# Unit 3's convolution moved from TensorE to the tap-by-tap path of the other units

## The chip, the cores and the metric

The kernel runs on one core of a Trainium2 chip. The metric is device time of one execution in microseconds (us); of several runs the median is given. A profile is one more execution, recorded by the hardware. Engines are named as in the profile: PE (TensorE matmuls), PEld (its weight loads), DVE (VectorE), ACT (ScalarE), POOL (GpSimd), SP (the sync engine, which only issues DMAs here).

## The reference

`x` has 8 sequences of 4096 tokens with 192 channels. First a causal convolution over 7 tokens: each of 8 heads has 24 channels and 7 weights, which are softmaxed. Then a gated feed-forward layer over all 32768 tokens:

```
w = exp(weight - max); w = w / (sum(w) + 1e-9)          # 8 x 7
y[b, s, h, :] = sum over k of w[h, k] * x[b, s + k - 6, h, :]
g = y @ w_gate; val = y @ w_val                          # 192 -> 1536
out = (g * sigmoid(g) * val) @ w_out                     # 1536 -> 192, float32
```

## The kernel before

**The main loop.** The 32768 tokens are cut into 64 blocks of 512, and the 1536 hidden features into 12 chunks of 128. One step is one chunk of one block, so there are 768 steps. A step `n` does six matmuls in `gate_val` (two halves of 64 rows for gate and val, three slices of the 192 channels), a SiLU on ACT (`sig`, L789) out of the gate's PSUM bank, and a product with val on DVE (`h`, L791). Gate and val have three PSUM banks each. Every third step a `slot` does 24 matmuls of the down projection (L806) on `h` of earlier steps; once a block, ACT and DVE copy the two result banks to `o_sb` and SP stores them.

**Where the convolved input comes from.** `gate_val` needs the convolved block with channels in partitions. Four blocks make a unit of 2048 tokens (48 steps); there are 16 units, 0 to 15. There are three ways to make them:

- Unit 0 (`early`): convolved on PE and turned in part on PE.
- Units 1 and 3: x is loaded in float16 windows of tokens by the POOL queue (`x16_tile`, `load_x`, L98) and duplicated by SP (`dup_x`, L148). `conv_half`, twice a unit, runs 32 matmuls (L476, 64 x 32 tiles of the array) between two groups of a slot's down projection, and casts the banks to `tm` on ACT and DVE (L493). POOL copies 64 channels (`conv_dup`, L504), SP stores `tm` to DRAM (`conv_out`) and fetches it transposed (`fetch`, L534).
- Units 2 and 4 to 15 (the tuple `POOLED`): channel-major, tap by tap. A DMA on the POOL queue casts the unit's x into DRAM as float16 (`cast_x`, L590). SP fetches it transposed, two tiles of 128 channels per block (`turn_x`, L605); the tiles of two blocks are joined for the last 64 channels (`join_x`, L609). Six jobs a unit (`conv_job`: four blocks, two pairs) then do the seven taps: ACT three (L682), DVE two (L657), POOL two products (L647) and four adds (L632). SP puts the results into the tiles that the matmuls read (`place`, L706, four DMAs a block).

**What sets the order.** All engines run a fixed order, written step by step in the loop; `seq` keeps it. For the pooled units `planned(v)` writes into `plan` at which step the cast, the ten turns and joins, and the jobs of unit `v` are handed out. Jobs go to one queue for ACT and one for DVE. `pooled_work` takes from them only in steps with `j` of 1, 7 or 10 (ACT also at 4, and twice at 10 in even blocks), and takes nothing in a step that holds `conv_half`: in four blocks that is at most 12 DVE taps and 18 ACT taps, which is what one unit needs. POOL's part of a job is issued when its DVE and ACT taps are. A block is placed when both its jobs were issued some steps ago and at the earliest 16 steps ahead of it:

```
if n < max(done + (12 if u == 2 else 18), ustep * u + NCH * i - 16):
```

**Buffers.** Tiles come from rings: `x01` and `x12` 8, `pxc0` 8, `pxc1` and `pxc2` 4, `total` 5, `part` 8, `y2` 4, the cast's DRAM buffer `xs` 2, `x16` 2. An instruction that would write a buffer still in use waits, and holds up what stands behind it on its engine or queue.

Of the kernel before, what the change touches and what calls it, by code (L numbers as in the profile page):

```python
# [10 lines left out]
def kernel(  # L11
# [11 lines left out]
    fp16 = mybir.dt.float16  # L23
# [7 lines left out]
    B, S, D = x.shape  # L31
# [3 lines left out]
    P = 128  # L35
# [10 lines left out]
    NG = 10  # L46
# [3 lines left out]
    ER = ((0, 3), (3, 5))  # L50
    XW = 2 * EG * EO
    NU = NT // UT
    POOLED = (2, *range(4, NU))
    upb = S // UT
    n_blocks = NT // TB
    n_steps = n_blocks * NCH
# [25 lines left out]
    cpool = ctx.enter_context(tc.tile_pool(name="conv", bufs=2))  # L82
# [41 lines left out]
    x16 = {}  # L124

    def x16_tile(u):
        x16[u] = cpool.tile([P, 4 * NG, D], fp16, tag="x16", name="x16")

    def load_x(u, r, after=None, low=0):
        t, t0, w0, p0 = x16[u], u * UT, 4 * NG * r, Q * r + low  # L130
# [90 lines left out]
    xe_tile(3)  # L221
    xe_load(3)
    x16_tile(1)
    for r in range(2):
        for low in (0, 32):
# [132 lines left out]
    def make_band():  # L358
        for r in range(2):
            for a in range(2):  # L360
                p0 = Q * r + 32 * a
                p1 = Q * r
                seq(
                    nc.gpsimd.tensor_copy(
                        band[p0 : p0 + 32], wide[p1 : p1 + 32, a, :, 0:32]
                    )
                )
# [208 lines left out]
    def cast_x(u):  # L576
        rows = XP + UT
        xs[u] = dpool.tile([rows, D], fp16, tag="xs", name="xs")
        flat = xs[u].rearrange("t d -> (t d)")
        skip = XP if u % upb == 0 else 0  # L580
        if skip:
            seq(
                nc.sync.dma_start(
                    out=flat[0 : XP * D].rearrange("(a n) -> a n", n=P),
                    in_=fill[0 : XP * D // P, :],
                )
            )
        n = (rows - skip) * D // P
        seq(
            nc.gpsimd.dma_start(  # L590
                out=flat[skip * D : rows * D].rearrange("(a n) -> a n", n=n),
                in_=bass.AP(
                    tensor=x_flat.tensor,
                    offset=(u * UT - XP + skip) * D,
                    ap=[[n, P], [1, n]],
                ),
            )
        )

    def turn_x(u, i, at):  # L600
        rows = xs[u][TB * i : TB * i + TB + XP]
        tiles = (x01, x12)[at // Q]
        tag = f"x{at // Q}"
        t = cpool.tile([P, TB + XP], fp16, tag=tag, name=tag, bufs=8)
        seq(nc.sync.dma_start_transpose(out=t, in_=rows[:, at : at + P]))  # L605
        tiles[u, i] = t

    def join_x(u, i):
        seq(nc.sync.dma_start(out=x12[u, 2 * i + 1][0:Q], in_=x12[u, 2 * i][Q:P]))  # L609
# [98 lines left out]
    def pooled(u):  # L708
        return u in POOLED

# [3 lines left out]
    def queue_jobs(u):  # L714
        for job in (
            ("block", 0), ("pair", 0), ("block", 1),
            ("block", 2), ("pair", 1), ("block", 3),
        ):
            conv_job(u, *job)
        placing.extend((u, i) for i in range(UB))  # L720

    def planned(v):
        s0 = ustep * v
        turns = (
            (0, 0), (0, Q), (1, Q), None, (1, 0), (2, 0), (2, Q), (3, Q), None, (3, 0)
        )
        if v == 2:
            cast, jobs = 21, 55
            times = (36, 36, 36, 38, 39, 39, 41, 41, 43, 43)
        elif v == 3:  # L730
            cast, jobs = 60, 56
            times = range(66, 86, 2)
        else:
            cast, jobs = s0 - 115, s0 - 89
            times = range(s0 - 105, s0 - 85, 2)
        plan.setdefault(cast, []).append(lambda: cast_x(v))
        for m, turn in enumerate(turns):
            if turn:
                todo = lambda turn=turn: turn_x(v, *turn)
            else:  # L740
                todo = lambda i=m // 8: join_x(v, i)
            plan.setdefault(times[m], []).append(todo)
        plan.setdefault(jobs, []).append(lambda: queue_jobs(v))
# [151 lines left out]
    make_band()  # L895
    for v in POOLED:
        planned(v)

    for n in range(n_steps):
        b, j = divmod(n, NCH)  # L900
        u, ls = divmod(n, ustep)
# [50 lines left out]
        if u + 2 < NU and not pooled(u + 2):  # L952
            if ls == (21 if u == 0 else 1):
                x16_tile(u + 2)
                load_x(u + 2, 0, silu[n - 1])
            if ls == (23 if u == 0 else 5):
                load_x(u + 2, 1, silu[n - 1])
            if ls == (37 if u == 0 else 26):
                dup_x(u + 2)
# [44 lines left out]
```

## Time and profile before

| What | Value |
|---|---|
| Time, median of 3 runs | 775.95 us (775.26 to 776.23) |
| Profiled execution | 775.12 us, of it 773.3 us span from the first to the last instruction |
| Granted TensorE clock | 1.00 |
| One half of `conv_half`, PE matmuls | 32, 0.67 us together |
| ACT tap, DVE tap | 715 ns, 1064 ns mean |
| POOL product, add of an ACT part, add of a product | 916 ns, 1271 ns, 1424 ns mean |
| Casts in DRAM (`xs`) | 13, of 768 or 774 KB, median 7 us to landing |

Views of the profile have one line for a group of like instructions or for a few in a row. In a list in order of time a line begins with start and length in us, then engine, source line, operation, what it writes and reads, and how many; what stands in brackets is how long the engine was idle before it and what ended that. "SPq" and "POOLq" are queues that issue DMAs: their lengths are the time to issue. A stretch by engine gives the busy time of PE, PEld, DVE, ACT and POOL in that order with the numbers of instructions, then the clock, the share of the DMA engines and GB/s.

### The profile page before, as it was taken

How to read it: one execution, taken by the hardware profiler on the slowest of the kernel's cores; microseconds unless marked ns; L12 is line 12 of the kernel's file. 1: busy time of each engine (PE TensorE's matmuls, PEld its weight loads, DVE VectorE, ACT ScalarE, POOL GpSimd, SP SyncE). 2: the span in 40 equal slices, each digit the busy share in tenths (PEclk: the TensorE clock that was granted, in tenths of full speed). 3: DMA queues.
4: the chain of work that ended last, by engine and by line, in shares of the span. 5: the costliest groups of instructions: out<-in, count | busy, mean ns of one | idle time of the engine just before them, and what ended most of it. 6: DMA issues, size and time to landing. Idle time of an engine off the chain costs nothing.

```text
span 773.3 us, 27884 instructions
## 1 busy us (share of the span) xinstructions
PE 766.8 (99%) x11179; PEld 645.5 (83%) x11179; DVE 688.9 (89%) x1034; ACT 636.8 (82%) x1093; POOL 578.8 (75%) x525
## 2 busy tenths in 40 slices
PE   8999999999999999999999999999999999999997
PEld 5666686668888888888888888888888888888886
DVE  7677998899999999999999999999999999997775
ACT  6667888888888888888888888888888888886664
POOL 8100796799989999898989989999899998882000
PEclk9999999999999999999999999999999999999999
DMA  9959855854635436355363543627454352221211
GB/s 134 190 125 135 169 118 108 158 105 101 115 96 113 107 86 106 89 118 115 77 119 84 109 101 80 123 78 122 88 111 111 87 121 74 56 70 39 67 57 42
DMA packets 143652, 79.32 MB, mean 103 GB/s; under 512 B 89146, under 2 KB 143042, under 8 KB 143042
## 3 DMA queue, kind: packets, MB, share of 16 engines
q1 hardware_dynamic: 130690, 61.58, 36.3%
q0 software_dynamic: 12832, 15.96, 13.3%
q8 instruction: 87, 1.43, 0.8%
q14 instruction: 43, 0.35, 0.2%
HBM read 31.92 MB, written 37.83 MB: 90 GB/s over the span
## 4 chain that ended last, share of the span: by engine, by line
PE 99%; ACT 0%; DVE 0%; issue 0%
PE gate L780 47%; PE acc L806 33%; PE val L780 18%; PE warm L880 0%; PE turn L445 0%; PE cv L476 0%; PE cv L387 0%; PE acc L827 0%; ACT tme L405 0%; ACT wide L345 0%; ACT o_sb L972 0%; PE taps L332 0%; DVE spread L312 0%; PE ctap L565 0%; DVE tap L310 0%
## 5 line engine op out<-in xcount | busy, mean ns | idle before, releaser
L791 DVE TENSOR_TENSOR h<-sig,val 128x512 f16<-128x512 f16 x768 | 498.8, 684 | 75.3 <-PE gate L780 51.8
L789 ACT ACTIVATE sig<-gate 128x512 f16<-128x512 f32 x768 | 458.2, 597 | 120.1 <-PE gate L780 71.8
L780 PE MATMUL gate<-pxc,w 64*128 64x512 f16 x1872 | 437.7, 376 | 0.0
L780 PE MATMUL val<-pxc,w 64*128 64x512 f16 x1872 | 437.6, 376 | 0.0
L780 PEld LDWEIGHTS <-w 64*128 64x128 f16 x4608 | 366.1, 110 | 85.2 <-issue 0.9
L806 PEld LDWEIGHTS <-h 64*128 64x128 f16 x6096 | 286.8, 94 | 29.4 <-issue 1.4
L806 PE MATMUL acc<-wo,h 64*128 64x192 f16 x6096 | 308.5, 243 | 0.0
L632 POOL TENSOR_TENSOR total<-total,part 128x512 f32<-128x512 f32 x156 | 198.3, 1271 | 64.7 <-DVE total L657 47.4
L657 DVE SCALAR_TENSOR_TENSOR total<-x,both_taps,total 128x512 f32<-128x512 f16 x156 | 166.0, 1064 | 0.0
L647 POOL TENSOR_SCALAR piece<-x,both_taps 128x512 f32<-128x512 f16 x156 | 142.9, 916 | 0.0
L632 POOL TENSOR_TENSOR total<-total,piece 128x512 f32<-128x512 f32 x78 | 111.1, 1424 | 6.5
L682 ACT ACTIVATE part<-x,both_taps 128x512 f32<-128x512 f16 x156 | 111.5, 715 | 0.0
L780 PE MATMUL val<-xc,w 64*128 64x512 f16 x432 | 102.0, 376 | 0.0
L780 PE MATMUL gate<-xc,w 64*128 64x512 f16 x432 | 101.9, 376 | 0.0
L632 POOL TENSOR_TENSOR pxc<-total,piece 128x512 f16<-128x512 f32 x52 | 66.8, 1285 | 4.3
L682 ACT ACTIVATE total<-x,both_taps 128x512 f32<-128x512 f16 x78 | 55.8, 716 | 0.0
L632 POOL TENSOR_TENSOR y<-total,piece 128x512 f16<-128x512 f32 x26 | 33.1, 1274 | 2.2
L864 DVE COPY o_sb<-acc 128x384 f32<-128x384 f32 x63 | 34.6, 549 | 0.0
L863 ACT COPY o_sb<-acc 128x384 f32<-128x384 f32 x63 | 29.8, 473 | 4.5 <-PE acc L806 4.5
L98 POOL DMA_DIRECT2D x<-in_x_dram x6 | 5.1, 871 | 24.4 <-ACT sig L789 24.4
L504 POOL COPY tm<-tm 128x1280 f16<-128x1280 f16 x2 | 2.5, 1252 | 17.3 <-DVE tm L493 17.3
L590 POOL DMA_DIRECT2D xs<-in_x_dram x13 | 7.2, 557 | 0.0
(67 smaller groups left out, 74.3 us busy)
## 6 DMA issues: line engine op xcount, KB each, us to landing
out_dram<-o_sb SPq DMA_DIRECT2D x63, 384.0 KB
pxc<-pxc SPq DMA_DIRECT2D x104, 64.0 KB
pxc<-y SPq DMA_DIRECT2D x104, 64.0 KB
xs<-in_x_dram POOLq DMA_DIRECT2D x7, 768.0 KB, 7.1
xs<-in_x_dram POOLq DMA_DIRECT2D x6, 774.0 KB, 6.8
x<-in_x_dram POOLq DMA_DIRECT2D x6, 480.0 KB, 10.1
scr<-tm SPq DMA_DIRECT2D x14, 130.0 KB
x<-x SPq DMA_DIRECT2D x26, 66.0 KB
```

Of the source, the lines that this page charges most:

```text
L98: nc.gpsimd.dma_start(out=t[p0 + i0 : p0 + i1, w0 - at : w1 - at, :], in_=bass.AP(tensor=x_flat.tensor, offset=(t0 + size * w0 - pad + i0) ...
L590: nc.gpsimd.dma_start(out=flat[skip * D : rows * D].rearrange("(a n) -> a n", n=n), in_=bass.AP(tensor=x_flat.tensor, offset=(u * UT - XP ...
L632: nc.gpsimd.tensor_tensor(job["dst"] if k == K - 1 else total, total, part, op=ALU.add)
L647: nc.gpsimd.tensor_scalar(part, shifted(k), scalar1=job["tap"][:, k : k + 1], scalar2=1.0, op0=ALU.mult, op1=ALU.mult,)
L657: nc.vector.scalar_tensor_tensor(job["total"], shifted(k), job["tap"][:, k : k + 1], job["total"], op0=ALU.mult, op1=ALU.add,)
L682: nc.scalar.activation(part, shifted(k), AF.Copy, scale=job["tap"][:, k : k + 1])
L780: nc.tensor.matmul(o, w16[m][p0 : p0 + Q, k, e::E], xc[b][k][p0 : p0 + Q, 0:TB], start=(k == 0), stop=(k == SL - 1),)
L789: silu[n] = seq(nc.scalar.activation(sg, g, AF.Silu)).ins
L791: seq(nc.vector.tensor_tensor(hj, sg, v, op=ALU.mult))
L806: nc.tensor.matmul(acc[b][bank][:, s, :], hj[p0 : p0 + Q, ts(2 * bank + s, P)], wo16[p0 : p0 + Q, j, :], start=(not second and j == 0 and ...
L863: seq(nc.scalar.copy(o_sb[:, 0:2, :], acc[b][0]))
L864: seq(nc.vector.tensor_copy(o_sb[:, 2:4, :], acc[b][1]))
```

## The change

Unit 3 joins the pooled units, so `conv_half`, `load_x`, `dup_x`, `conv_out` and `fetch` remain for unit 1 alone, and `x16` needs one buffer. The jobs of unit 2 are handed out at step 46 in place of 55. The branch of `planned` for unit 3 (cast at step 60, turns at 66 to 84, jobs at 56, behind those of unit 2 in the queues) stood in the code before and is now used. For units from 4 on, the turns and joins are handed out 95 to 77 steps ahead of the unit in place of 105 to 87.

```
-    POOLED = (2, *range(4, NU))
+    POOLED = range(2, NU)
...
     def x16_tile(u):
-        x16[u] = cpool.tile([P, 4 * NG, D], fp16, tag="x16", name="x16")
+        x16[u] = cpool.tile([P, 4 * NG, D], fp16, tag="x16", name="x16", bufs=1)
...
         if v == 2:
-            cast, jobs = 21, 55
+            cast, jobs = 21, 46
             times = (36, 36, 36, 38, 39, 39, 41, 41, 43, 43)
         elif v == 3:
             cast, jobs = 60, 56
             times = range(66, 86, 2)
         else:
             cast, jobs = s0 - 115, s0 - 89
-            times = range(s0 - 105, s0 - 85, 2)
+            times = range(s0 - 95, s0 - 75, 2)
```

## The prediction

> **What bounds the kernel now.** I read the busy shares first, then the chain of work that ended last, then TensorE in order of time around unit 3's convolution. After that I read the engines that the change loads: stretches by engine, and ScalarE and the sync queue in order of time where the margins are small.
>
> ```profile
> PE 766.8 (99%) x11179; PEld 645.5 (83%) x11179; DVE 688.9 (89%) x1034; ACT 636.8 (82%) x1093; POOL 578.8 (75%) x525
> PE 99%; ACT 0%; DVE 0%; issue 0%
> ```
>
> TensorE is busy for 766.8 of 773.3 us and is 99% of the chain, so only TensorE time counts, and a new wait that TensorE feels. The other engines are hidden as long as they deliver in time. The next view is TensorE in order of time, with the gate and val matmuls between left out (each line: start, length, engine, line, operation, count).
>
> ```profile
> 112.36 1.21 PE L806 MATMUL acc<-wo,h 64*128 64x192 f16 x24
> 115.29 1.21 PE L806 MATMUL acc<-wo,h 64*128 64x192 f16 x24
> 118.22 0.71 PE L806 MATMUL acc<-wo,h 64*128 64x192 f16 x12
> 118.87 0.67 PE L476 MATMUL cv<-x,band 64*32 64x240 f16 x32
> 119.47 0.67 PE L806 MATMUL acc<-wo,h 64*128 64x192 f16 x12
> ...
> 121.92 0.82 PE L806 MATMUL acc<-wo,h 64*128 64x192 f16 x15
> ```
>
> Three steps of the main loop take 115.29 - 112.36 = 2.93 us, and again 118.22 - 115.29 = 2.93. The three that hold half of unit 3's convolution take 121.92 - 118.22 = 3.70. The starts of the gate matmuls in the whole trace say the same: after step 39 every group of three steps takes 2.93 us except the two with unit 3's convolution, 3.697 each. So from step 39 on there are only two irregularities, and the change removes both.
>
> **What goes.** Two halves of unit 3's convolution, 32 matmuls each. Each half costs 3.697 - 2.933 = 0.764 us of TensorE, together 1.53 us. The 0.67 us length of one matmul group bounds it from below (2 x 0.67 = 1.34), and the period difference, which also holds the switch of tile shape and the stop between, is the upper end. I take the period difference because the period is what repeats. Also gone with unit 3, all hidden before: 8 casts on DVE and ACT (0.65 and 0.56 us each), a copy on POOL (1.25 us), two loads of 480 KB on the POOL queue, two duplications, nine stores and twelve transposes on SP. Their cover was the TensorE period, so they give nothing by themselves.
>
> **What comes.** Unit 3 now takes 18 ScalarE taps (0.715 us), 12 DVE taps (1.064), 6 x 4 adds and 6 x 2 products on POOL, a cast in DRAM, 8 transposes, 2 joins and 16 placements on SP. That is what every unit from 4 on already issues, and this row shows what that costs:
>
> ```profile
> 140.00:600.00 460.00, 460.00 (x6594) 400.42 (x6590) 433.74 (x628) 401.30 (x687) 416.68 (x362) 1.00 0.50 104
> ```
>
> The columns after the stretch are its length, then PE, PEld, DVE, ACT and POOL busy. Over 460 us DVE is 94% busy and POOL 91%, and the period stays 2.93 us. One unit is 48 steps = 46.9 us. Its POOL work is 6 jobs x (2 x 1.27 + 2 x 0.92 + 1.42 + 1.28) = 42.5 us, and the loop hands out exactly 12 DVE and 18 ScalarE slots in 48 steps. So a fourteenth unit fits, but nothing catches up any more: the lead that unit 2 starts with is the lead of all. Counting the loop's rules, unit 2's first tap moves from step 58 to 49, unit 3's stands at 97, unit 4's moves from 109 to 145 and every later unit runs 33 steps later than before. The last tap moves from step 685 to 718. The tightest placement in steady state comes 11 steps (10.8 us) before its block, as unit 2's third and fourth did before (steps 109 and 121 for 120 and 132), and those blocks began on time. Cost 0. Without this cover each us of late placement would be a us of time.
>
> A rule speaks against this part. "SBUF — State Buffer" of the Trainium skill, section "Who interferes with whom", says that a DVE instruction with two SBUF inputs and a GpSimd instruction that reads SBUF lock each other out for a whole instruction. If each of the 12 added taps waited for one whole POOL add of 1.27 us, DVE would have 12 x 0.75 + 12 x 1.27 = 24.2 us of taps in unit 3's 46.9 us beside 48 products (0.65 apart, 31.2) and four copies (2.2): 57.6 us, 10.7 too many, and the time would be about 785. The trace agrees on the contention (a DVE tap takes 0.75 us beside an idle POOL, up to 1.6 beside a busy one), but the mean is 1.06, and the sum goes by that.
>
> **What moves 10 steps back.** The ten transposes and joins of each later unit pass at most one output store and one placement each on SP. They now stand 95 to 77 steps ahead of their unit and its first tap 47, so all are 30 or more steps early. The cast that they read is issued 20 steps ahead of the first of them in place of 10 (9.8 us, against a landing of 7.1), so SP waits less for it. Cost 0.
>
> **Where it is tight: unit 2 at steps 49 and 58.** ScalarE now needs unit 2's first tile at step 49 and its first pair tile at step 58, both 9 and 6 steps earlier than before, and sigmoids of the main loop stand behind these taps in ScalarE's order. ScalarE, then SP, then POOL's waits, before:
>
> ```profile
> 61.41 1.89 ACT L789 ACTIVATE sig<-gate 128x512 f16<-128x512 f32 x3 [1.04 <-PE val L780]
> 64.34 1.89 ACT L789 ACTIVATE sig<-gate 128x512 f16<-128x512 f32 x3 [1.04 <-PE val L780]
> ...
> 71.99 0.72 ACT L682 ACTIVATE total<-x,both_taps 128x512 f32<-128x512 f16 x1
> 72.61 0.71 ACT L682 ACTIVATE part<-x,both_taps 128x512 f32<-128x512 f16 x1
> ```
>
> ```profile
> 59.62 4.85 SPq L605 DMA_TRANSPOSE x<-xs  x3
> 64.57 4.03 SPq L534 DMA_TRANSPOSE xc<-scr  x3
> 70.60 0.55 SPq L609 DMA_DIRECT2D x<-x  x1
> ```
>
> ```profile
> 62.95 0.86 POOL L98 DMA_DIRECT2D x<-in_x_dram  x1 [21.68 <-ACT sig L789]
> 66.53 0.84 POOL L98 DMA_DIRECT2D x<-in_x_dram  x1 [2.71 <-ACT sig L789]
> ```
>
> Step 49's tap comes after the sigmoids that end at 63.3 us. The semaphore records of the first transpose are complete at 62.97, and ScalarE has 1.04 us idle there, 0.4 more than a tap adds (72.61 - 71.99 = 0.62). So it fits. Step 58 takes two taps from 72.0 on, the first of them on the joined pair. Before, the join was issued at 70.60 and landed at 76.9: that would be 4.9 us late. But what delayed it is unit 3's load, which goes: transposes issued at 55.7 to 61.9 landed 2.6 to 2.8 us later, the one issued at 63.22, after the load's first half, only at 70.56, and those issued at 71 at 77; once the load's second half was in (76.5), it is 2.7 to 3.4 us again. Without the load the source of the join lands at about 65.9, SP reaches the join right after the three transposes of 64.57 (68.6) instead of waiting until 70.6, and it lands some 2 us later (84.58 to 86.5 is the row for a join alone), at 70.6 to 71.2. That is 0.8 to 1.4 us ahead. Cost 0, with 4.9 us less the 0.6 that the sigmoid behind can give away, 4.3 us, as the upper end.
>
> **Sum.** 0 + 0 + 0 - 1.53 us. The profiled execution took 775.12 us (span 773.3 and 1.8 around it) and would take 773.6. It lies 0.8 us under the median of the runs shown, so I forecast 775.95 - 1.53 = 774.4 us. That is a gain of 0.197%, right at the 0.2% that a measurement of this kernel can tell from no change.
>
> **Rivals.**
> - *The join stays late (other side).* If the transposes themselves, not the load, slow the queue, the tap at step 58 waits in ScalarE until the join is in, and the sigmoids, then the gate banks, then TensorE wait with it. Each us of landing after 72.6 costs one; from 74.1 on the kernel is slower, and with the old landing it is 775.95 - 1.53 + 4.3 = 778.7. Against it speak the landings above. Chance 0.09.
> - *Unit 2's first placement comes late.* Unit 3's cast stands on POOL behind unit 2's first job (before from 82.4 to 90.0 us, now nine steps, 8.8 us, sooner: 73.6 to 81.2), lands 7 to 10 us after its issue at 81.2, at 88.9 to 91.8, and SP waits for it with the transposes of unit 3. Six of them (7.6 us), a join wait and a store lie before the placement, so it is issued at 98.4 to 101 and lands after another 5 to 7, against the need at 108.1. Lateness of at most about 1 us eats most of the gain: 775.3. For it speaks that POOL's next cast comes into the same stretch; against it that the same neighbours stood there before and the block began on time. Chance 0.10.
> - *A small wait at step 49.* The tile lands up to 1 us later in some executions; ScalarE's slack and the three gate banks take most of it. 774.7. Chance 0.05.
> - *No new wait, 774.4*: 0.76, with 773.7 to 775.2 as its own range (the runs shown lie within 1 us of each other).
>
> **How the numbers follow.** The case without a new wait falls about evenly on both sides of the 0.2% bound, because its gain is the bound: 0.41 faster, 0.35 within. The late placement and the wait at step 49 give 0.11 within, 0.03 faster and 0.01 slower; the late join gives 0.08 slower and 0.01 within. Faster 0.44, same 0.47, slower 0.09. The range runs from 773.4 to 775.9, past the second rival, and leaves out the late join and some scatter.
>
> **What will show it.** Right: no convolution rows of unit 3, all groups of three steps at 2.93 us from step 39 on, TensorE busy about 1.5 us less. Wrong: a group over 2.95 us at steps 48 to 60 (ScalarE's tap waiting for a transpose or join), or at steps 96 to 108 with TensorE waiting for a placement; or later, every 48 steps, which would mean that the lost lead mattered.

## The result and the profile after

| | before | after |
|---|---|---|
| Median of 22 runs each | 775.89 us | 777.70 us |
| Lowest to highest | 775.03 to 776.68 | 775.51 to 781.19 |
| Profiled execution, span | 775.12, 773.3 | 776.99, 775.2 |
| TensorE clock in it | 1.000 | 0.998 |

The ratio is 1.0027, 95% interval 1.0016 to 1.0038: slower by 0.27%, where 0.2% faster was forecast. The executions also scatter over 5.7 us where they scattered over 1.7.

The page after, busy shares and chain:

```profile
PE 767.7 (99%) x11115; PEld 566.6 (73%) x11115; DVE 698.3 (90%) x1042; ACT 645.6 (83%) x1107; POOL 618.0 (80%) x559
PE 98%; POOL 0%; ACT 0%; DMA 0%; DVE 0%; issue 0%; SPq 0%; POOLq 0%
PE val L780 50%; PE acc L806 33%; PE gate L780 13%; PE warm L880 1%; PE turn L445 0%; POOL total L632 0%; PE cv L387 0%; PE acc L827 0%; DMA pxc<-pxc 0%; PE cv L476 0%; ACT tme L405 0%; SPq L706 0%; DVE total L657 0%; DVE h L791 0%; ACT wide L345 0%
```

TensorE has 64 matmuls fewer and is no less busy, and a placement (`SPq L706`) with its DMA (`pxc<-pxc`) has come into the chain that ended last. By the starts of the gate matmuls, the two long groups with unit 3's convolution (3.70 us each) are gone, and a new one stands at steps 96 to 98: 6.97 us in place of 2.93. These are the first steps of unit 2's first block. TensorE in order of time there:

```profile
108.13 0.38 PE L780 MATMUL gate<-pxc,w 64*128 64x512 f16 x1
108.18 0.38 PE L780 MATMUL val<-pxc,w 64*128 64x512 f16 x1
109.43 0.37 PE L780 MATMUL gate<-pxc,w 64*128 64x512 f16 x1 [0.88 <-DMA pxc<-pxc]
110.11 0.37 PE L780 MATMUL val<-pxc,w 64*128 64x512 f16 x1 [0.31 <-DMA pxc<-y]
110.71 0.44 PE L780 MATMUL gate<-pxc,w 64*128 64x512 f16 x1 [0.23 <-DMA pxc<-y]
111.38 0.58 PE L780 MATMUL val<-pxc,w 64*128 64x512 f16 x1 [0.24 <-DMA pxc<-pxc]
```

The block's first slice needs no placement and starts on time at 108.13. The other four reads each wait for one of the four placing DMAs, 1.66 us in all. The stretches around it, after and then before (length, PE, PEld, DVE, ACT, POOL busy, then the clock):

```profile
108.00:112.00 4.00, 2.35 (x13) 0.84 (x11) 1.65 (x3) 1.19 (x2) 3.83 (x5) 0.86 0.44 98
112.00:140.00 28.00, 28.00 (x386) 21.04 (x383) 24.64 (x36) 22.89 (x39) 20.65 (x19) 0.96 0.47 113
```

```profile
108.00:112.00 4.00, 4.00 (x56) 3.34 (x54) 3.71 (x7) 3.10 (x6) 3.92 (x4) 1.00 0.53 107
112.00:140.00 28.00, 28.00 (x446) 19.77 (x444) 24.32 (x39) 23.65 (x42) 19.48 (x18) 1.00 0.55 117
```

Before, the clock was 1.00 in both. After, 0.14 x 4 + 0.04 x 28 = 1.7 us are lost to it. So the 4.04 us of the group are 1.66 of waiting, 1.7 of slower clock, and some 0.7 that no row names, where the slices ran one by one between the waits.

Why the placement was late stands in SP's order, after:

```profile
82.64 4.86 SPq L605 DMA_TRANSPOSE x<-xs  x1
87.61 1.89 SPq L867 DMA_DIRECT2D out_dram<-o_sb  x2
89.59 4.57 SPq L605 DMA_TRANSPOSE x<-xs  x3
95.63 0.47 SPq L609 DMA_DIRECT2D x<-x  x1
96.15 1.39 SPq L605 DMA_TRANSPOSE x<-xs  x1
97.65 0.52 SPq L867 DMA_DIRECT2D out_dram<-o_sb  x1
98.21 6.38 SPq L605 DMA_TRANSPOSE x<-xs  x1
104.63 0.55 SPq L583 DMA_DIRECT2D xs<-fill  x1
105.23 2.12 SPq L605 DMA_TRANSPOSE x<-xs  x1
107.40 0.57 SPq L706 DMA_DIRECT2D pxc<-pxc  x1
```

and in POOL's, where the casts of units 3 and 4 are issued:

```profile
80.69 0.57 POOL L590 DMA_DIRECT2D xs<-in_x_dram  x1
97.10 0.55 POOL L590 DMA_DIRECT2D xs<-in_x_dram  x1
```

A transpose usually takes SP 1.25 to 1.3 us to issue. The one at 82.64, 2 us after a cast, takes 4.86, and the one at 98.21, 1 us after the next, takes 6.38: SP stands until about the time when the cast lands (87.4 and 104.9 us). These are no waits for a semaphore: in the profile's list of SP's waits from 80 to 110 us, where the longest is 1.8 us for a join, the transposes do not stand. What holds SP inside the instruction was not found out. The placement behind it is issued at 107.40. Before, SP's order was this:

```profile
95.05 0.99 SPq L706 DMA_DIRECT2D pxc<-pxc  x1
97.20 1.14 SPq L706 DMA_DIRECT2D pxc<-y  x2
98.39 2.92 SPq L706 DMA_DIRECT2D pxc<-pxc  x1
104.21 1.83 SPq L605 DMA_TRANSPOSE x<-xs  x1
```

The same cast (97.11 to 104.2 us there) was in flight and held the fourth placing DMA, though only until 101.3. The placement stood ahead of the next transposes and was out by then.

So the account of the trace is -1.53 + 4.04 = +2.5 us up to the last step, whose first gate matmul starts at 768.40 in place of 765.89; the span grew by 1.9, because the end of the last store came sooner after it in this execution.

### The profile page after: what moved, and what is told of

It is laid out like the page before. It is cut to its first block, busy times and chain, and to the rows that moved or that the text cites. A ratio compares the mean times of both kernels' runs of the same rounds, so it can differ in the third digit from the quotient of the medians.

```text
span 775.2 us, 27840 instructions
## 1 busy us (share of the span) xinstructions
PE 767.7 (99%) x11115; PEld 566.6 (73%) x11115; DVE 698.3 (90%) x1042; ACT 645.6 (83%) x1107; POOL 618.0 (80%) x559
## 4 chain that ended last, share of the span: by engine, by line
PE 98%; POOL 0%; ACT 0%; DMA 0%; DVE 0%; issue 0%; SPq 0%; POOLq 0%
PE val L780 50%; PE acc L806 33%; PE gate L780 13%; PE warm L880 1%; PE turn L445 0%; POOL total L632 0%; PE cv L387 0%; PE acc L827 0%; DMA pxc<-pxc 0%; PE cv L476 0%; ACT tme L405 0%; SPq L706 0%; DVE total L657 0%; DVE h L791 0%; ACT wide L345 0%
## 5 line engine op out<-in xcount | busy, mean ns | idle before, releaser
L780 PE MATMUL gate<-pxc,w 64*128 64x512 f16 x2016 | 472.4, 376 | 1.1 <-DMA pxc<-pxc 0.9
L780 PE MATMUL val<-pxc,w 64*128 64x512 f16 x2016 | 472.3, 376 | 0.5 <-DMA pxc<-y 0.3
L780 PEld LDWEIGHTS <-w 64*128 64x128 f16 x4608 | 316.8, 110 | 165.7 <-issue 4.2
L806 PE MATMUL acc<-wo,h 64*128 64x192 f16 x6096 | 339.1, 243 | 0.0
L806 PEld LDWEIGHTS <-h 64*128 64x128 f16 x6096 | 306.7, 94 | 31.1 <-issue 1.2
L632 POOL TENSOR_TENSOR total<-total,part 128x512 f32<-128x512 f32 x168 | 213.3, 1270 | 82.8 <-DVE total L657 60.9
L657 DVE SCALAR_TENSOR_TENSOR total<-x,both_taps,total 128x512 f32<-128x512 f16 x168 | 179.9, 1071 | 0.0
L647 POOL TENSOR_SCALAR piece<-x,both_taps 128x512 f32<-128x512 f16 x168 | 154.9, 922 | 0.0
L780 PE MATMUL val<-xc,w 64*128 64x512 f16 x288 | 68.2, 376 | 0.0
L780 PE MATMUL gate<-xc,w 64*128 64x512 f16 x288 | 68.1, 377 | 0.0
```

Of the source, the lines that this page charges most:

```text
L632: nc.gpsimd.tensor_tensor(job["dst"] if k == K - 1 else total, total, part, op=ALU.add)
L647: nc.gpsimd.tensor_scalar(part, shifted(k), scalar1=job["tap"][:, k : k + 1], scalar2=1.0, op0=ALU.mult, op1=ALU.mult,)
L657: nc.vector.scalar_tensor_tensor(job["total"], shifted(k), job["tap"][:, k : k + 1], job["total"], op0=ALU.mult, op1=ALU.add,)
L780: nc.tensor.matmul(o, w16[m][p0 : p0 + Q, k, e::E], xc[b][k][p0 : p0 + Q, 0:TB], start=(k == 0), stop=(k == SL - 1),)
L806: nc.tensor.matmul(acc[b][bank][:, s, :], hj[p0 : p0 + Q, ts(2 * bank + s, P)], wo16[p0 : p0 + Q, j, :], start=(not second and j == 0 and ...
```

## The experiments

Theory A: one late placement makes the whole loss, its cause is a cast in flight that holds SP's transposes (A1: unit 4's; A2: unit 3's already), and the rest of the change is free. Rival B: the fourteenth unit on POOL, DVE and ACT, or the lost lead, costs time in many places. Theory C: part of the loss is the clock that falls after the wait. Ratios are to the kernel before, run on the same chip beside each. Every profile counts from its own first instruction. By the first row of unit 1's convolution (37.8 us before and after and with the early placement, 38.4 with either cast moved and with both placements ahead, 38.6 with the jobs alone, 39.0 with the transposes back) the main loop stands 0 to 1.2 us later in it; differences between kernels are taken after that is subtracted.

### Place unit 2 earlier

```
-            if n < max(done + (12 if u == 2 else 18), ustep * u + NCH * i - 16):
+            lag, lead = (8, 21) if u == 2 else (18, 16)
+            if n < max(done + lag, ustep * u + NCH * i - lead):
```

> The changed kernel, but unit 2's blocks may be placed 8 steps after their jobs and 21 steps ahead of the block, in place of 12 and 16: the first placement stands at step 75, two transposes of unit 3 sooner on SP. Theory A (that one placement was late because SP stood in transposes that a cast held up; all the rest of the change is free): the placement is issued at about 97.6 us, lands by 105, steps 96 to 98 take 2.93 us as all others, clock 1.00, time 774.4 us, ratio to the kernel before 0.998. Rival B (the fourteenth unit on POOL, DVE and ACT, or the lost lead, costs time in many places): it stays at 776.5 to 778.

Measured: 773.89 us (772.76 to 775.35), ratio 0.9977 (0.9969 to 0.9986). After step 39 every group takes 2.93 us. SP:

```profile
97.86 0.53 SPq L706 DMA_DIRECT2D pxc<-pxc  x1
98.49 5.57 SPq L706 DMA_DIRECT2D pxc<-y  x2
104.12 0.58 SPq L706 DMA_DIRECT2D pxc<-pxc  x1
```

One edit to the order on SP gives back the whole loss and the forecast gain. B falls: this kernel does all the added work. The placing DMAs are held by the cast too (5.57 us for two), so it is not a matter of transposes alone; they are merely early enough.

### Issue unit 4's cast later

```
-            cast, jobs = s0 - 115, s0 - 89
+            cast, jobs = s0 - (105 if v == 4 else 115), s0 - 89
```

> The changed kernel, but unit 4's cast is issued 10 steps later (step 87). Theory A1 (unit 4's cast, in flight from 97.1 to 104.2 us, holds up SP's transpose of 6.4 us at 98.2): that transpose takes 1.3 us, the placement is issued at about 102 and lands by 105 to 106, no TensorE wait, 774.4 us. Rival A2 (unit 3's own cast, which SP waits for until 89.6 us, has already made it late): the placement gains less than 3 us, TensorE still waits, 776 us or more. Rival B: 776.5 to 778.

Measured: eight executions at 772.99 to 774.07 us, four at 778.80 to 780.44; median 773.64, ratio 0.9998 (0.9976 to 1.0019). The profile is of one at 773.44:

```profile
90.34 4.49 SPq L605 DMA_TRANSPOSE x<-xs  x3
96.37 0.47 SPq L609 DMA_DIRECT2D x<-x  x1
96.88 1.27 SPq L605 DMA_TRANSPOSE x<-xs  x1
98.26 0.52 SPq L867 DMA_DIRECT2D out_dram<-o_sb  x1
98.83 2.67 SPq L605 DMA_TRANSPOSE x<-xs  x2
101.60 0.54 SPq L706 DMA_DIRECT2D pxc<-pxc  x1
```

The expectation gives the cast's flight as in the kernel before (to 104.2 us); in the changed kernel it lands at 104.9. With the 0.6 us of this profile subtracted, SP comes to unit 3's transposes at 89.7, as in the changed kernel (89.59), so unit 3's cast costs as much as there. But with no cast in flight the last two transposes take 2.67 us together, and the placement is issued at 101.0 in place of 107.40, which is enough. (0.55 us of that gain is the small store of `fill`, which `cast_x` issues on SP and which moves along.) That is A1. The four long executions were not expected. Their mean clock is 0.995 to 0.998, that of the other eight 0.999 or 1.000; the last experiment asks for them.

### Issue unit 3's cast earlier

```
-            cast, jobs = 60, 56
+            cast, jobs = 57, 56
...
+        if after is not None:
+            tc.add_manual_dep(i.ins, after.name, SYNC, reason="cast in turn")
```

(`after` is the SiLU of step 56, for unit 3 alone.)

> The changed kernel, but unit 3's cast is issued before unit 2's first job on POOL, after the SiLU of step 56, at about 71.5 us in place of 80.7. Theory A2 (the cast behind POOL's job makes SP wait): it lands by 79 to 80, SP reaches the placement at about 95, before unit 4's cast, and it lands by 101; no TensorE wait, 774.4 us. Rival A1 (only unit 4's cast matters): the placement still falls into its flight, 775.5 to 778. What can go wrong: unit 2's last transposes and the fetch for block 7 meet the earlier cast.

Measured: 777.78 us (775.32 to 780.25), ratio 1.0025 (1.0010 to 1.0039), as slow as the change. The cast is issued at 71.72, and SP:

```profile
76.47 6.90 SPq L534 DMA_TRANSPOSE xc<-scr  x3
...
91.21 4.56 SPq L607 DMA_TRANSPOSE x<-xs  x3
...
99.79 6.38 SPq L607 DMA_TRANSPOSE x<-xs  x1
...
108.96 0.57 SPq L708 DMA_DIRECT2D pxc<-pxc  x1
```

The earlier cast holds other instructions, among them the fetch for block 7 (its three transposes take 6.90 us together), and SP reaches unit 3 no sooner (91.21, or 90.6 with the 0.6 subtracted). So A2's gain could not show, and this run alone doesn't tell A1 from A2. It does show that a cast moved on POOL takes its hold on SP along. Steps 66 to 68 lost 0.6 us as well.

### Dummy matmuls in the place of the wait

```
+        if n == 96:
+            dummy = ppool.tile([P, TB], fp32, tag="gate", name="dummy")
+            for _ in range(14):
+                seq(nc.tensor.matmul(dummy, fill, fill.unsqueeze(1).to_broadcast([P, SUBS, P]), ...))
         gate_val(n)
```

> The changed kernel with 14 dummy matmuls (128x512, some 3.0 us) on TensorE ahead of step 96, so that TensorE works instead of waiting for the placement; nothing is left out. Theory C (about 2.3 us of the 4.0 lost at step 96 is the wait, the rest is the granted clock, which falls to a half for 3.4 us after the wait): clock 1.00 throughout, no wait of over 0.3 us at step 96, the profile's span 771.7 + 3.0 = 774.7 us, time 776.5 to 777.4, with a spread of 1 us or less over the executions in place of nearly 6. Rival D (the clock drop has another cause): the clock still drops, and the time is 778 or more.

Measured: 777.26 us (776.09 to 778.16), ratio 1.0022 (1.0013 to 1.0031); the profile has clock 1.000, a span of 774.3 and no wait at step 96:

```profile
108.16 3.19 PE L918 MATMUL dummy<-fill 128*128 128x512 f16 x14
111.29 0.40 PE L780 MATMUL gate<-pxc,w 64*128 64x512 f16 x1
```

The added work cost 3.4 us against the early placement (777.26 - 773.89). By the ratios that cannot be told from the price of the wait that it covers: the intervals of 1.0022 here and 1.0027 (1.0016 to 1.0038) for the changed kernel overlap. In the two profiles the groups of steps lost 3.29 us here and 4.04 there. The scatter falls from 5.7 to 2.1 us, not to 1 as expected. The 22 executions of the changed kernel fit: nine with a mean clock of 0.999 or 1.000 took 775.5 to 777.4 us, seven with 0.997 or 0.998 took 777.0 to 779.7, six with 0.995 took 779.3 to 781.2, and 0.005 of 778 us is 3.9 us. C holds in its main point: with TensorE kept busy the clock stays up and most of the scatter goes. In the profile of the changed kernel the wait alone was 1.66 of the 4.04 us.

### The two other parts, each alone in the kernel before

Jobs of unit 2 at step 46:

```
-            cast, jobs = 21, 55
+            cast, jobs = 21, 46
```

> The kernel before with one part of the change alone: the jobs of unit 2 at step 46 in place of 55; unit 3 stays on TensorE with its loads. Theory E (the joined pair is late for step 58 as long as unit 3's loads are in flight beside it, as the prediction's first rival priced it): ScalarE's tap of step 58 waits from 72.0 to about 76.9 us for the join, TensorE stands for about 4 us at steps 60 to 63 and loses up to 2 us of clock after it: 779 to 782 us. Rival F (the buffers between ScalarE and TensorE take it up, or the join lands sooner): 775.7, as the kernel before.

Measured: 781.60 us (781.23 to 782.28), ratio 1.0081 (1.0068 to 1.0094). ScalarE, then TensorE:

```profile
70.86 1.89 ACT L789 ACTIVATE sig<-gate 128x512 f16<-128x512 f32 x3 [0.43 <-PE val L780]
77.47 0.72 ACT L682 ACTIVATE total<-x,both_taps 128x512 f32<-128x512 f16 x1 [4.71 <-DMA x<-x]
```

```profile
79.34 1.75 PE L806 MATMUL acc<-wo,h 64*128 64x192 f16 x24 [4.28 <-ACT sig L789]
```

Theory E's wait holds to 0.2 us: ScalarE waits 4.71 us for the join, TensorE 4.28 for the SiLU behind it, and steps 60 to 65 take 6.1 us more than they should; the clock, 0.997 on the mean, takes the rest. In the changed kernel, without unit 3's loads, the join was issued at 68.72 and the same tap started without a wait:

```profile
68.72 0.54 SPq L609 DMA_DIRECT2D x<-x  x1
71.99 0.71 ACT L682 ACTIVATE total<-x,both_taps 128x512 f32<-128x512 f16 x1
```

So the earlier jobs are only possible because unit 3 leaves the windowed path. That it is the loads which matter is argued from the landings in the prediction; no run took the loads away alone.

Transposes of later units 10 steps back:

```
-            times = range(s0 - 105, s0 - 85, 2)
+            times = range(s0 - 95, s0 - 75, 2)
```

> The kernel before with one part of the change alone: the transposes and joins of units from 4 on 10 steps later. Every theory so far: all of them are still 4 or more steps ahead of their taps, no wait, 775.7 us, within 0.1% of the kernel before. Only if the transposes then meet placements in SP's order could TensorE wait: each such place would show as a group of steps over 2.95 us.

Measured: 775.70 us, ratio 1.0002 (0.9994 to 1.0011). No difference, as expected.

### Both placements ahead of the trouble, with and without the 10 steps

```
-            times = range(66, 86, 2)
+            times = range(72, 92, 2)
...
+            lag, lead = (8, 30) if u == 2 else (18, 16)
+            if n < max(done + lag, ustep * u + NCH * i - lead):
```

> The changed kernel with the two first placements of unit 2 ahead of unit 4's cast or right behind it: unit 3's transposes 6 steps later (steps 72 to 90), unit 2's blocks placed 8 steps after their jobs and up to 30 steps ahead. Theory A: the first placement is issued at 92 to 95 us, ahead of the cast at 97.1, the second by 107; no TensorE wait in any execution, every group after step 39 takes 2.93 us; time 773.9 us (the kernel before less 1.5 to 1.9), the spread under 2 us, narrower than with the early placement alone (2.6). Rival B: not under 775.

Measured: 773.58 us (772.71 to 774.00), ratio 0.9973 (0.9965 to 0.9982), the best here. SP:

```profile
93.08 0.58 SPq L706 DMA_DIRECT2D pxc<-pxc  x1
93.70 1.24 SPq L706 DMA_DIRECT2D pxc<-y  x2
94.98 0.59 SPq L706 DMA_DIRECT2D pxc<-pxc  x1
...
107.46 0.53 SPq L706 DMA_DIRECT2D pxc<-pxc  x1
```

In this profile unit 4's cast is issued at 97.73: the first placement is out before it, the second soon after it has landed. With the 0.6 us subtracted they are 5.4 and 8.8 us sooner than with the early placement alone (97.86 and 115.68). The scatter is 1.3 us in place of 2.6.

The same with `range(s0 - 105, s0 - 85, 2)` for the later units:

> The kernel of e8_before_cast4 with the third part of the change undone: transposes of later units 105 to 87 steps ahead again. If the shift by 10 steps was needed: SP waits in the last transposes of every unit for tiles that taps of two units before still read (some 2 to 4 us a unit), and the placements behind them come late, 775 or more. If it was not: the same 773.9 as e8_before_cast4.

Measured: 775.18 us (772.88 to 781.08), ratio 0.9997 (0.9981 to 1.0013). One wait in the profile, at step 120:

```profile
134.47 0.37 PE L781 MATMUL val<-pxc,w 64*128 64x512 f16 x1 [0.98 <-DMA pxc<-pxc]
```

The group with this wait took 4.11 us, 1.18 more than the others, and the clock stayed at 1.00 in the 6 us after it. In this kernel the 10 steps are worth 1.6 us by the medians, though the two intervals just touch (0.9981 and 0.9982), and not for the reason expected. No unit after that waits; it is unit 2's third block, whose placement (128.65 us) now stands behind unit 4's transposes on SP.

### Later cast and early placement together

> The kernel of e2_cast4_late (unit 4's cast 10 steps later) with the early placement rule for unit 2 (8 steps after the jobs, up to 30 ahead). It asks what made 4 of 12 executions of e2_cast4_late take 779 to 780 us. Theory G (there the second placement, issued at 113.8 to 117.5 us against a need at about 119.5, was late in some executions, and the wait cost clock too): with the second placement issued by about 107 no execution is over 775 and the median is 773.6. Rival H (something else in the later cast, as unit 4's transposes behind it): some executions stay at 779 to 780.

Its edit is that of the later cast plus the rule with (8, 30). Measured: 773.71 us, seven executions between 773.29 and 773.81, ratio 0.9974 (0.9963 to 0.9985). None is long, as theory G says. But at a rate of 4 in 12, seven short ones in a row come by chance in about one case of 17 ((2/3)^7 = 0.06), and the edit moves unit 2's first placement too, not only the second. So that the second placement came late in the long executions of the later cast is likely and not shown; none of them was profiled.

## Why the prediction was wrong

- **The bound and the gain** were right. TensorE's period sets the time, unit 3's convolution was 1.53 us, and with no wait left (both placements ahead) the last step starts 726.6 us after unit 1's convolution in place of 728.1. Measured against the median, that kernel gains 0.27% (0.18 to 0.35%), which holds the forecast 0.197%.
- **The fourteenth unit** is free, as the sum said: a DVE tap takes 1.07 us on the mean as before (1071 ns and 1064), and the rule on the port that DVE and GpSimd share, weighed there, added nothing to it.
- **The first rival** (the join late at step 58) did not come, for the reason given: with unit 3 gone the join was issued at 68.7 and ScalarE's tap started at 71.99 without a wait. With unit 3's loads in place TensorE's wait was 4.28 us, where 4.3 was priced, but the time rose by 5.9, since the clock fell too.
- **A small wait at step 49** came, 0.43 us in ScalarE, and cost TensorE nothing.
- **The second rival is what happened, and its sizing is the step that failed.** "Six of them (7.6 us), a join wait and a store lie before the placement, so it is issued at 98.4 to 101": each transpose was put at 1.27 us, the median of all. Behind a cast the fifth of them took 6.38, and the store of the fill (0.55 us) was left out. The placement was issued at 107.40. The row that shows such a hold was in the profile of before: the fourth placing DMA took SP 2.92 us at 98.39, right after the cast. The argument "the same neighbours stood there before and the block began on time" overlooked that the placement stood ahead of those neighbours then. A second term erred the other way: the landing was put at another 5 to 7 us, and here, with the cast landed, each read started 2.0 to 2.1 us after its DMA was issued (the first at 109.43). With 5 to 7 us it would have started at 112.4 or later.
- **The price of a wait was too low.** "Lateness of at most about 1 us eats most of the gain: 775.3" takes a us of lateness as a us of time and leaves out the clock. The wait of 1.66 us took 4.04, 1.7 of it by the clock.

The Trainium skill, "TensorE: Matmul & The Clock Gate", section "Part 1: The HAM clock gate", puts the halved clock after at least one idle window of about 3.4 us. Here no single gap was longer than 0.88 us. The slices lengthen from the one at 110.71 on (0.44, then 0.58 us in place of 0.37), so the three gaps before it, 1.42 us in all between 108.56 and 110.71, were enough, and the measurement decides.

## What to carry to other kernels

When a step moves on a queue that issues DMAs, price everything that it is now behind at the rate which the queue has while the largest transfer near it is in flight, not at its usual rate. Put what TensorE waits for ahead of what is needed tens of steps later, even if both seem early. And price a wait of a busy TensorE above its length: 1.66 us cost 4.0 here and 4.28 cost 6.1, because the clock fell after it, and the time scattered. A single wait of 0.98 us cost 1.18 and left the clock at 1.00.

## What the runs showed that was not expected

- A cast from DRAM to DRAM on POOL's queue (768 or 774 KB, about 7 us) stops SP's issue, not only the landing of its DMAs: transposes that take 1.27 us otherwise took 4.86 and 6.38, two placing DMAs 5.57, three fetches 6.90. The hold went along when the cast was moved. Why it holds SP stays open, and it need not last until the landing: before, the DMA of 98.39 was through at 101.3, with the cast in flight until 104.2.
- Gaps of 1.42 us within 2.2 us (1.66 us of waits in all) brought TensorE's granted clock to 0.86 in that stretch of 4 us and 0.96 in the next 28, about 1.7 us of time; dummy matmuls in the same place kept it at 1.000.
- Here a wide scatter went with a margin that was used up: 5.7 us over the executions with the late placement, 1.3 us with both placements well ahead.
